# Batch 2's first two head pairs turned by transposing transfers instead of TensorE, in an attention and mixer kernel

## The chip, the cores and the metric

The kernel runs on one core of a Trainium2 chip. The metric is the device time of one execution in microseconds. The core has TensorE (PE; its weight loads are listed as PEld), VectorE (DVE), ScalarE (ACT), GpSimd (POOL) and SyncE (SP). In this kernel POOL issues the loads from memory, which also turn float32 into bfloat16, and SP issues stores, small copies and transposing transfers.

## The reference

The reference is causal attention with a decay bias, followed by a mixer block. There are 8 batches, 8 heads, 576 positions and 64 channels per head.

```python
scores = scale * np.matmul(q, k.transpose(0, 1, 3, 2))
cum = np.cumsum(np.maximum(s, 0.0), axis=-1)
bias = -(cum[:, :, :, None] - cum[:, :, None, :])
scores = np.where(causal, -1000000000.0, scores + np.minimum(bias, 0.0))
attn = softmax(scores)
x = np.matmul(attn, v)                # then heads side by side: (8, 576, 512)
...
h = x.transpose(0, 2, 1) @ U @ V      # U (576, 32), V (32, 576)
u = x + h.transpose(0, 2, 1)
out = u + np.maximum(u @ w_ch1, 0.0) @ w_ch2    # (512, 2048), (2048, 512)
```

## The kernel before

The 64 heads are worked off in 32 pairs (n = 0 to 31), four pairs to a batch; pair n belongs to batch n // 4. For each pair q and k have to stand with the 64 channels on partitions. They are put into a tile of `slots`, with four more rows that carry the running sums of s, so that one matmul yields scores and bias together. `slot_of` names the tile: for pairs 8 and up it is (n + 1) % 3 of the first three, so pair 8 uses slots[0] and pair 9 slots[1], which pairs 5 and 6 used before.

The words of the order are these. T is the filling of a slot, S the scores with their exponentials, V the product with v and its normalisation, M the low-rank mixing of a batch, F a step of the channel mixer, and D a transposing transfer of a pair. The channel mixer (`chanmix`) runs as `fill`: after most steps of attention `step_fill` gives it a turn, at a pace. PE and POOL run in the order of the program text (`in_program_order` at the end); the order on VectorE, ScalarE and SP is set by it up to the first batch and by the planner after that.

There are two ways to fill a slot.

- `transposes` (L301): q and k of a batch were loaded by `load_qk` (L128) with 72 partitions, in pieces of 512 numbers, into one of the two operand tiles `qk_sd` (even batches the first, odd ones the second). PE turns each pair with 16 matmuls against the identity (L316: two heads, q and k, four pieces) into PSUM, and four copies (L335) spread the result into the slot. `copies` gives some of them to ScalarE: of pairs 8 and 9, those of the first head.
- `turn_pair` and `part_pair` (L349, L358): `load_pair` (L117) brings q and k of one pair with 96 partitions, in four loads of pieces of 64 numbers, into a quarter of the second operand tile (`of_pair`). `turn_pair` has SP issue a transposing transfer (L350) into one of three `landings`: a tile of its own called `turned`, the rest of the second operand tile, and the head of the first one. Then it calls `load_pair` for the pair four further on. `part_pair` copies the two halves of the landing into the slot on VectorE (L362).

In both, from batch 1 on, `rows_of` has SP fetch the bias rows into the slot by two small transfers (L296) ahead of the rest.

`ZP` is the first pair that goes the second way: 10 before. So batch 2's pairs 8 and 9 are loaded by `load(2)` (heads 0 to 3 into the first operand tile, which batch 0 has left) and turned by PE; pairs 10 and up go through transfers. The words around it (L1240 on):

```python
weave("S5 T6 S5 F T6 S5 F S5 S6 T7 S6 T7 S6 S6")
for n in range(ZP, ZP + PB):
    load_pair(n)
weave("V4 V4 S7 V5 S7 V5 S7 V6 S7 V6 T8 T8 V7 S8 V7 S8 T9 S8 T9 D10")
weave("S8 S9 M1 S9 D11 M1 S9 D12 M1 M1 S9 M1 F M1")
```

The last PE reads of the second operand tile as batch 1's operand are those of T7, so the loads of a pair into it wait for them.

Of the kernel before, what the change touches and what calls it, by code (L numbers as in the profile page):

```python
# [41 lines left out]
def kernel(  # L42
# [15 lines left out]
    B, H, S, D = q.shape  # L58
# [7 lines left out]
    NP = BH // 2  # L66
    PB = NP // B
# [2 lines left out]
    KA = D + 4  # L70
    NF = FF // 128
    FT = 2
    ZB, ZP = 3, 10
    TR, RT = 96, 6

    consts = ctx.enter_context(tc.tile_pool(name="consts", bufs=1))
# [10 lines left out]
    def pwork():  # L87
        return ps_w.tile([128, 512], FP32, tag="w", name="pwork")
# [17 lines left out]
    qk_sd = [consts.tile([128, 2 * H * TT * D], BF16, name=f"qk_sd{i}") for i in range(2)]  # L106
    QK = 2 * PB * RT * 128

    def alloc_qk(b):
        q_t[b], k_t[b] = qk_sd[b % 2][:TP].rearrange("p (c h x) -> c p h x", c=2, h=H)  # L110

    def of_pair(n):
        return qk_sd[ZB % 2][:TR, ds(n % PB * QK // PB, QK // PB)].rearrange(
            "p (c t two d) -> p c t two d", c=2, t=RT, two=2
        )

    def load_pair(n):  # L117
        b, hp = divmod(n, PB)
        for hh in range(2):
            for c, src in enumerate((q, k)):  # L120
                nc.gpsimd.dma_start(  # L121
                    out=of_pair(n)[:, c, :, hh, :],
                    in_=src[b, 2 * hp + hh].rearrange("(t p) d -> p t d", p=TR),
                )

    def load_qk(b, h, n):
        for dst, src in ((q_t[b], q), (k_t[b], k)):
            nc.gpsimd.dma_start(  # L128
                out=dst[:, ds(h, n), :],
                in_=src[b, ds(h, n)].rearrange("h (p t) d -> p h (t d)", p=TP),  # L130
            )
# [32 lines left out]
    def init_v(eng, vt):  # L164
        eng.memset(vt[64:, 4, :, :], 0.0)
        eng.memset(vt[:, 0:4, :, D : D + 1], 1.0)
        eng.memset(vt[0:64, 4, :, D : D + 1], 1.0)

    def v_slot(b):
        return v_slots[b % 3 if b < 3 else 2 - b % 2]  # L170

    def load_v(b, parts=range(5)):
        vt = v_slot(b)
        if 0 < b < 3:
            init_v(nc.gpsimd, vt)
        for t in parts:
            rows_t = 128 if t < 4 else 64
            nc.gpsimd.dma_start(  # L178
                out=vt[:rows_t, t, :, 0:D],
                in_=v[b, :, ds(t * 128, rows_t), :].rearrange("h p d -> p h d"),  # L180
            )
# [10 lines left out]
    def slot_of(n):  # L192
        return slots[n % NSLOT if n < 2 * PB else (n + 1) % 3]
# [93 lines left out]
    def copies(n, hh, par):  # L287
        b = n // PB
        on_act = hh == (n in (4, 7)) and (
            n in (0, 4, 7, 8, 9) or (n, par) == (1, 0)  # L290
        )
        return nc.scalar.copy if on_act else nc.vector.tensor_copy

    def rows_of(n):
        for r, n_r, c in ((0, 3, 1), (3, 1, 0)):
            nc.sync.dma_start(  # L296
                out=slot_of(n)[ds(D + r, n_r), :, ds(c * S, S)],
                in_=rows_hbm[ds(r, n_r), ds(2 * n, 2)],
            )

    def transposes(n):  # L301
        b, hp = divmod(n, PB)
        slot = slot_of(n)
        if b > 0:
            rows_of(n)
        tps = {}

        def turn(hh, c):
            if c == 0:
                tile = pwork()  # L310
                tps[hh] = tile.bitcast(BF16)[:, : 2 * 4 * TP].rearrange(
                    "p (c t m) -> p c t m", c=2, t=4
                )
            src = (q_t[b], k_t[b])[c]
            for t2 in range(4):
                nc.tensor.transpose(  # L316
                    tps[hh][:, c, t2, :],
                    src[:, 2 * hp + hh, ds(t2 * 128, 128)],
                    identity[:TP, :TP],
                )  # L320

        if b == 0:
            for hh in range(2):
                turn(hh, 0)
            yield
        for hh in range(2):
            if b > 0:
                turn(hh, 0)
            turn(hh, 1)
            tp = tps[hh]  # L330
            dst = slot[0:D, hh, 0 : 2 * S]
            for par in range(2):
                src = tp[par * D : par * D + D]
                in_turn = dst.rearrange("p (c m t two) -> p c m t two", c=2, t=4, two=2)
                copies(n, hh, par)(in_turn[:, :, :, :, par], src.rearrange("p c t m -> p c m t"))  # L335
            yield
# [7 lines left out]
    def last_sp():  # L344
        return [ins for ins in list(nc.cur_bb.bb.instructions) if ins.engine == E.SP][-1]
# [3 lines left out]
    def turn_pair(n):  # L349
        nc.sync.dma_start_transpose(  # L350
            out=landing(n).rearrange("p (a m) -> p a m", m=TR),
            in_=of_pair(n).rearrange("p c t two d -> p (c t two d)"),
        )
        after(tc, last_sp(), x_turned[-1])
        if n < NP - PB:
            load_pair(n + PB)
# [728 lines left out]
    def step_fill():  # L1085
        pace[0] += pace[1]
        if pace[0] < 16:
            return
        pace[0] -= 16
        if NG - 3 in expanded and not ps_tail:  # L1090
            return
        while fill:
            if next(fill[0], fill) is not fill:
                return
            fill.pop(0)
# [9 lines left out]
    def fill_with(n):  # L1105
        per, pace[1] = pace[1], 16
        for _ in range(n):
            step_fill()
        pace[1] = per


    def pT_of(n):
        if n < PB + 3:
            return pTs[n % 2] if n % PB < 2 else pT_early[n % PB - 2]
        return pTs[(n + 1) % 2]

    def step(*gens):
        for gen in gens:
            next(gen, None)
# [75 lines left out]
    load_v(1)  # L1195
    load_w2(1)

    def load(b):
        alloc_qk(b)
        load_qk(b, 0, 4)  # L1200

    load(2)
    load_v(2)
    fill.append(chanmix(0, first_hT, 4))
    pace[1] = 0
    made = {}

    def weave(order):
        for word in order.split():
            if word == "F":  # L1210
                fill_with(1)
                continue
            kind, n = word[0], int(word[1:])
            if kind == "D":
                x_turned.append(last_sp())
                turn_pair(n)
                x_turned.pop()
                continue
            if word not in made:
                if kind == "T":  # L1220
                    made[word] = transposes(n)
                elif kind == "S":
                    made[word] = scores(n, pT_of(n))
                elif kind == "V":
                    made[word] = values(n, pT_of(n))
                else:
                    made[word] = seqmix(n)
            step(made[word])
            step_fill()
# [8 lines left out]
        nc.vector.tensor_copy(V_end[ds(dt * R, R), dt, :], V_sb[:R, 512:S])  # L1238
    pace[1] = 7
    weave("S5 T6 S5 F T6 S5 F S5 S6 T7 S6 T7 S6 S6")  # L1240
    for n in range(ZP, ZP + PB):
        load_pair(n)
    weave("V4 V4 S7 V5 S7 V5 S7 V6 S7 V6 T8 T8 V7 S8 V7 S8 T9 S8 T9 D10")
    weave("S8 S9 M1 S9 D11 M1 S9 D12 M1 M1 S9 M1 F M1")
    fill.append(chanmix(1))
    pace[1] = 11
    for n in range(2 * PB, NP + 2):
        b, hp = divmod(n, PB)
        if hp == 0 and b + 1 < ZB:
            load(b + 1)  # L1250
        if ZP + 3 <= n + 3 < NP:
            turn_pair(n + 3)
        mixing = seqmix(b - 1) if hp == 1 and b > FT else iter(())
        if b == B:
            fill_with(3)
            for _ in range(3):
                step(mixing)
                fill_with(2)
        if n > 2 * PB and n + 1 < NP:
            for at, _ in enumerate((transposes if n + 1 < ZP else part_pair)(n + 1)):  # L1260
                step_fill()
                if at == 1:
                    step(mixing)
        if 2 * PB + 1 < n < NP:
            for at, _ in enumerate(scores(n, pT_of(n))):
                relu_by[0] = E.DVE if hp == 1 and at == 2 else E.Activation
                step_fill()
                relu_by[0] = E.Activation
                if at == 1:
                    step(mixing)  # L1270
        for _ in mixing:
            fill_with(1)
        if hp == 1 and FT < b < B:
            fill.append(chanmix(b - 1))
            pace[1] = 12 if b < 6 else 10
        if 2 * PB < n <= NP:
            run(values(n - 1, pT_of(n - 1)))
        if 2 <= b < B - 1:
            if b + 1 < ZB:
                load_v(b + 1, range(5 if hp == 0 else 0))  # L1280
            else:
                load_v(b + 1, ((0, 1), (2,), (3,), (4,))[hp])
# [70 lines left out]
```

## Time and profile before

| | |
|---|---|
| median of 3 runs | 348.08 us (347.5 to 348.23) |
| profiled execution | 348.07 us, its span 346.4 us |
| granted TensorE clock | 1.0 |
| PE transposes, L316 | 160 weight loads (98 ns) and 160 matmuls (198 ns) |
| copies from PSUM, L335 | 29 on VectorE (803 ns), 11 on ScalarE (801 ns) |
| copies from a landing, L362 | 44 on VectorE (455 ns) |
| transposing transfers of pairs, L350 | 22, SP busy with issuing one for 1.28 to 3.10 us |
| loads of pairs on POOL, L121 | 88 of 72 KB, issued in 0.73 us each, median 4.3 to 4.4 us to landing |

The span is the time from the first to the last instruction of the program; the time of an execution has 1.7 us more around it. The transposes' lengths overlap in the engine: four groups of eight of them belong to pairs 8 and 9. "To landing" is the time from the issue of a transfer until its data has arrived.

### The profile page before, as it was taken

To read this page: it belongs to the slowest core of one execution; us is meant where nothing else is said; L and a number is where in the kernel's file an instruction comes from. 1 tells how busy PE (TensorE), PEld (TensorE's weight loads), DVE (VectorE), ACT (ScalarE), POOL (GpSimd) and SP (SyncE) were. 2 spreads that over 40 slices of the span, in tenths; PEclk is the share of its full clock that TensorE was granted. 3 is DMA by queue.
4 is the path that set the end of the run, shared out by engine and by line. 5 is a ranking of instruction groups with operands and counts; after the bars stand their busy time and mean duration, and the time that the engine had idled before them with its cause. 6 is when DMAs were issued, how large, how long until landed. Compare 5 with 4: busy or idle time off the path is not lost.

```text
span 346.4 us, 8956 instructions
## 1 busy us (share of the span) xinstructions
PE 336.5 (97%) x3623; PEld 243.8 (70%) x3657; DVE 259.3 (75%) x576; ACT 205.2 (59%) x310; POOL 123.6 (36%) x179
## 2 busy tenths in 40 slices
PE   8999999999999999999999999999999999999996
PEld 4585656655688558865678558865687558888885
DVE  8884756779799558974898459965989597875774
ACT  4886985838850886168724874378462546675710
POOL 7997454839476337322933274000000000000000
PEclk9999999999999999999999999999999999999999
DMA  7999999999999999999999999583025343010022
GB/s 106 159 179 207 186 186 120 129 204 189 154 162 174 202 126 127 114 206 151 124 116 168 163 135 143 117 177 76 2 70 122 69 83 71 32 61 32 30 93 91
DMA packets 166529, 43.79 MB, mean 126 GB/s; under 512 B 151129, under 2 KB 164857, under 8 KB 166489
## 3 DMA queue, kind: packets, MB, share of 16 engines
q0 software_dynamic: 97456, 18.44, 73.7%
q1 hardware_dynamic: 68744, 24.60, 35.7%
q8 instruction: 28, 0.46, 0.6%
q10 hardware_dynamic: 288, 0.20, 0.2%
q14 instruction: 13, 0.10, 0.1%
HBM read 37.25 MB, written 9.70 MB: 136 GB/s over the span
## 4 chain that ended last, share of the span: by engine, by line
PE 78%; DVE 9%; ACT 3%; issue 3%; DMA 3%; POOL 2%; DVEq 0%; ACTq 0%
PE pwork L662 23%; PE pwork L720 13%; PE quarter L720 10%; PE pscore L428 9%; PE pwork L492 7%; PE parts L952 6%; PE pwork L681 3%; DMA w_sb<-in_moe_w_ch_dram 3%; DVE uT L547 2%; DVE slot L698 1%; DVE o_sb L734 1%; POOL v_slot L178 1%; PE pscore L662 1%; ACT pT L446 1%; PE pwork L952 1%
## 5 line engine op out<-in xcount | busy, mean ns | idle before, releaser
L662 PE MATMUL pwork<-uT,w_sb 128*128 128x512 bf16 x407 | 104.2, 379 | 1.9 <-ACT pT L464 0.5
L1044 ACT ACTIVATE hT<-pwork 128x512 bf16<-128x512 f32 x107 | 64.7, 610 | 37.4 <-PE pwork L662 36.6
L446 ACT ACTIVATE pT<-pscore 128x1024 bf16<-128x1024 f32 x57 | 57.5, 1030 | 49.3 <-PE pscore L428 49.2
L662 PEld LDWEIGHTS <-w_sb 128*128 128x128 bf16 x448 | 39.1, 98 | 39.2 <-issue 1.0
L121 POOL DMA_DIRECT2D qk_sd<-in_q_dram x44 | 32.6, 740 | 75.4 <-DMA qk_sd<-qk_sd 48.4
L428 PE MATMUL pscore<-slot 68*128 68x128 bf16 (+1 forms) x506 | 55.9, 246 | 0.6 <-DMA slot<-hT 0.2
L428 PEld LDWEIGHTS <-slot 68*128 68x128 bf16 x570 | 42.0, 97 | 18.2 <-DMA slot<-hT 0.8
L720 PEld LDWEIGHTS <-hT 128*128 128x128 bf16 x496 | 46.8, 98 | 7.1 <-DVE uT L547 0.5
L372 DVE TENSOR_TENSOR pT<-pT,keep 128x512 bf16<-128x512 bf16 (+1 forms) x81 | 28.5, 353 | 28.7 <-ACT pT L446 22.4
L492 PEld LDWEIGHTS <-pT 128*128 128x128 bf16 x870 | 32.4, 98 | 6.1 <-issue 0.9
L492 PE MATMUL pwork<-v_slot,pT 128*128 128x65 bf16 x870 | 35.4, 193 | 0.2 <-DVE uT L547 0.2
L178 POOL DMA_DIRECT2D v_slot<-in_v_dram x40 | 34.5, 875 | 2.9 <-DMA w_sb<-in_moe_w_ch_dram 2.3
L121 POOL DMA_DIRECT2D qk_sd<-in_k_dram x44 | 32.4, 736 | 2.6 <-DMA v_slot<-in_v_dram 1.4
L502 DVE TENSOR_TENSOR x_sb<-pwork,rec 128x320 bf16<-128x320 f32 x64 | 31.1, 488 | 1.4
L458 ACT ACTIVATE pT<-pscore 128x1024 bf16<-128x1024 f32 x29 | 30.3, 1045 | 2.1 <-PE pscore L428 2.0
L720 PE MATMUL pwork<-w_sb,hT 128*128 128x256 bf16 x240 | 29.9, 272 | 0.0
L720 PEld LDWEIGHTS <-slot 128*128 128x128 bf16 x256 | 24.1, 98 | 4.1 <-issue 1.1
L335 DVE COPY slot<-pwork 64x576 bf16<-64x576 bf16 x29 | 23.3, 803 | 4.5 <-PE pwork L316 3.2
L501 DVE RECIPROCAL rec<-pwork 128x5 f32<-128x5 f32 x64 | 12.0, 188 | 12.8 <-PE pwork L492 12.4
L720 PE MATMUL pwork<-w_sum,slot 128*128 128x256 bf16 x160 | 20.1, 272 | 0.3 <-DVE o_sb L734 0.3
L720 PE MATMUL quarter<-w_sb,hT 128*128 128x256 bf16 x144 | 18.0, 273 | 0.3 <-DVE uT L547 0.3
L965 DVE TENSOR_TENSOR hT<-pT,parts 128x512 bf16<-128x512 f32 x16 | 10.8, 682 | 6.3 <-PE parts L952 3.6
(164 smaller groups left out, 491.4 us busy)
## 6 DMA issues: line engine op xcount, KB each, us to landing
out_dram<-o_sb SPq DMA_DIRECT2D x34, 256.0 KB
v_slot<-in_v_dram POOLq DMA_DIRECT2D x32, 128.0 KB, 6.6
w_sb<-in_moe_w_ch_dram POOLq DMA_DIRECT2D x4, 1024.0 KB, 13.5
qk_sd<-in_q_dram POOLq DMA_DIRECT2D x44, 72.0 KB, 4.4
qk_sd<-in_k_dram POOLq DMA_DIRECT2D x44, 72.0 KB, 4.3
qk_sd<-in_q_dram POOLq DMA_DIRECT2D x3, 288.0 KB, 10.5
qk_sd<-in_k_dram POOLq DMA_DIRECT2D x3, 288.0 KB, 10.7
qk_sd<-in_q_dram POOLq DMA_DIRECT2D x4, 144.0 KB, 4.8
```

Of the source, the lines that this page charges most:

```text
L121: nc.gpsimd.dma_start(out=of_pair(n)[:, c, :, hh, :], in_=src[b, 2 * hp + hh].rearrange("(t p) d -> p t d", p=TR),)
L178: nc.gpsimd.dma_start(out=vt[:rows_t, t, :, 0:D], in_=v[b, :, ds(t * 128, rows_t), :].rearrange("h p d -> p h d"),)
L372: nc.vector.tensor_tensor(dst, dst, keep[:, :, 0:w].to_broadcast([128, n_tiles, w]), op=ALU.min)
L428: nc.tensor.matmul(dst, lhsT=slot[0:KA, hh, ds(S + j * 128, 128)], rhs=slot[0:KA, hh, lo:hi], start=True, stop=True,)
L446: nc.scalar.activation(pT[:, hh, 0:1024], near, EXP, scale=scale)
L458: nc.scalar.activation(pT[:, :, 1024:1536], mid.rearrange("p (a b) -> p a b", a=2), EXP, scale=scale)
L492: nc.tensor.matmul(po[:, i, :], lhsT=pT[:, hh, ds(place(j, i), 128)], rhs=vt[:, j, h, :], start=(j == 0), stop=(j == i), skip_group_check= ...
L502: nc.vector.tensor_tensor(x_sb[:, hp, :, ds(hh * D, D)], po[:, :, 0:D], rec.to_broadcast([128, 5, D]), op=ALU.mult,)
L662: nc.tensor.matmul(f1, lhsT=w1_sb[:, kt, ds(nf * 128, 128)], rhs=u[:, kt, :], start=(kt == 0), stop=(kt == 3),)
L720: nc.tensor.matmul(acc[:, i, :], lhsT=a[:, kt, ds(i * 128, 128)], rhs=b[:, kt, :], start=(begin and i == 0 and kt == 0), stop=(kt == HF - ...
L952: nc.tensor.matmul(acc[:, i, :], lhsT=w[:, kt, ds((2 * e + i) * 128, 128)], rhs=m[:, kt, :], start=(begin and i == 0 and kt == 0), stop=(k ...
L1044: nc.scalar.activation(hT[:, nf, :], f1, RELU)
```

## The change

`ZP` becomes 8, so pairs 8 and 9 also go through `load_pair`, `turn_pair` and `part_pair`. Pair 8 is loaded into a place in the first operand tile (behind the first 1152 columns, which are a landing), pair 9 into its quarter of the second. `load(2)` is gone and `load_pair(8)` stands in its place; batch 2's v load moves from there to behind `load_pair(9)`, after T7. The loads of pairs 12 and 13, which stood in a loop, are now called by D8 and D9. D8 stands at the head of the order and D9 between the two steps of T8. The landings rotate by two places, since they count from `ZP`.

```diff
-    ZB, ZP = 3, 10
+    ZB, ZP = 3, 8
...
     def of_pair(n):
-        return qk_sd[ZB % 2][:TR, ds(n % PB * QK // PB, QK // PB)].rearrange(
-            "p (c t two d) -> p c t two d", c=2, t=RT, two=2
-        )
+        if n == ZP:
+            place = qk_sd[(ZB + 1) % 2][:TR, ds(2 * S, QK // PB)]
+        else:
+            place = qk_sd[ZB % 2][:TR, ds(n % PB * QK // PB, QK // PB)]
+        return place.rearrange("p (c t two d) -> p c t two d", c=2, t=RT, two=2)
...
         on_act = hh == (n in (4, 7)) and (
-            n in (0, 4, 7, 8, 9) or (n, par) == (1, 0)
+            n in (0, 4, 7) or (n, par) == (1, 0)
         )
...
-    def load(b):
-        alloc_qk(b)
-        load_qk(b, 0, 4)
-
-    load(2)
-    load_v(2)
+    load_pair(ZP)
...
-                    made[word] = transposes(n)
+                    made[word] = (transposes if n < ZP else part_pair)(n)
...
-    for n in range(ZP, ZP + PB):
+    load_pair(ZP + 1)
+    load_v(2)
+    for n in range(ZP + 2, ZP + PB):
         load_pair(n)
-    weave("V4 V4 S7 V5 S7 V5 S7 V6 S7 V6 T8 T8 V7 S8 V7 S8 T9 S8 T9 D10")
+    weave("D8 V4 V4 S7 V5 S7 V5 S7 V6 S7 V6 T8 D9 T8 V7 S8 V7 S8 T9 S8 T9 D10")
...
-        if hp == 0 and b + 1 < ZB:
-            load(b + 1)
-        if ZP + 3 <= n + 3 < NP:
+        if 2 * PB + 2 <= n < NP - 3:
             turn_pair(n + 3)
```

The order of the instructions on the engines is that of before but for this: PE has 32 weight loads and matmuls fewer, ScalarE four copies fewer, VectorE four copies of another kind in place of four (and one mask and one output sum beside them change places), POOL eight loads of pairs 8 and 9 in place of two of batch 2, ahead of batch 2's v loads, and SP two transposing transfers more. On SP, D8 stands ahead of the bias rows of pair 8, D9 between those of pairs 8 and 9, and D10 right behind the rows of pair 9, as before.

## The prediction

> **What bounds the kernel now.** I read the busy shares of the page first, then PE's order of time around batch 2's first head pairs, then the chain of waits there, then the queues that would have to feed the new path.
>
> ```profile
> span 346.4 us, 8956 instructions
> PE 336.5 (97%) x3623; PEld 243.8 (70%) x3657; DVE 259.3 (75%) x576; ACT 205.2 (59%) x310; POOL 123.6 (36%) x179
> ```
>
> PE is busy for 336.5 of 346.4 us, so whatever leaves PE's queue shortens the span, and whatever makes PE wait lengthens it: only 9.9 us of idle time exist in all, spread over the whole span, and nothing later can absorb a stall. The granted clock is full throughout. PE's own order of time shows what the change takes away:
>
> ```profile
> 57.49 0.62 PE L492 MATMUL pwork<-v_slot,hT 128*128 128x65 bf16 x15
> 57.95 0.43 PE L316 MATMUL pwork<-identity,qk_sd 72*128 72x72 bf16 x8
> 58.20 1.03 PE L681 MATMUL pwork<-w_sb,hT 128*128 128x512 bf16 x4
> 59.07 0.42 PE L316 MATMUL pwork<-identity,qk_sd 72*128 72x72 bf16 x8
> 59.33 0.62 PE L492 MATMUL pwork<-v_slot,pT 128*128 128x65 bf16 x15
> 60.08 0.62 PE L428 MATMUL pscore<-slot 68*128 68x128 bf16 x6
> ...
> 63.39 0.42 PE L316 MATMUL pwork<-identity,qk_sd 72*128 72x72 bf16 x8
> 63.65 0.60 PE L428 MATMUL pscore<-slot 68*128 68x320 bf16 x4
> ...
> 64.95 0.42 PE L316 MATMUL pwork<-identity,qk_sd 72*128 72x72 bf16 x8
> 65.21 0.23 PE L428 MATMUL pwork<-slot 68*128 68x64 bf16 x2
> ```
>
> The first column is the start, the second the length (ends overlap, so costs are read from start to next start). The four L316 groups are the transposes of pairs 8 (57.95, 59.07) and 9 (63.39, 64.95). The scores of pair 8 start at 60.08. The chain of waits says why:
>
> ```profile
> 58.43 0.79 issue
> 59.22 0.82 ACT slot L335
> 60.04 0.05 issue
> 60.08 0.62 PE pscore L428 x6
> ```
>
> The 15 matmuls at 59.33 need 0.46 us (57.49 to 57.95), so PE could have gone on at 59.79; it waited 0.29 us for ScalarE's second copy out of PSUM.
>
> Now the feeding side. The weight load ahead of batch 2's operands, the wait it causes on POOL, and the first transposing transfer of before (pair 10) on SP:
>
> ```profile
> 36.84 0.89 POOL L263 DMA_DIRECT2D w_sb<-in_moe_w_ch_dram  x1 [1.03 <-DMA qk_sd<-in_q_dram]
> 37.76 0.75 POOL L128 DMA_DIRECT2D qk_sd<-in_q_dram  x1
> 42.09 0.72 POOL L128 DMA_DIRECT2D qk_sd<-in_k_dram  x1 [3.58 <-PE pwork L662]
> 52.28 0.73 POOL L121 DMA_DIRECT2D qk_sd<-in_q_dram  x1 [3.97 <-DMA w_sb<-in_moe_w_ch_dram]
> ...
> 63.38 1.57 SPq L350 DMA_TRANSPOSE turned<-qk_sd  x1
> 65.06 1.36 SPq L296 DMA_DIRECT2D slot<-rows_hbm  x2
> 69.87 5.06 SPq L350 DMA_TRANSPOSE qk_sd<-qk_sd  x2
> ```
>
> The reader is to see a queue that runs ahead of its data: the weights issued at 36.84 land 14.9 us later, at 51.74, and POOL's next loads wait for such landings. From 42 to 63 us every POOL load that waits starts 0.2 to 0.8 us after the landing of the eighth load before it, so eight are in flight at most.
>
> **The change, part by part.**
>
> PE loses 32 transposes. Their four groups take 0.25 (57.95 to 58.20), 0.26, 0.26 and 0.26 us: 1.03 us. The rest of PE's order is unchanged, instruction by instruction, so this is a full gain. The 0.29 us wait for ScalarE's copy goes too. Without any new wait PE reaches pair 8's scores at 60.08 - 0.29 - 0.51 = 59.28 us.
>
> ScalarE loses four copies of 0.80 us. VectorE swaps four copies of 0.803 us for four of 64x1152 from SBUF (median 0.455). Both engines wait for PE in this stretch (3.39 of 5 us busy on ScalarE, 3.58 on VectorE from 55 to 60 us), so I count nothing for them.
>
> The new wait is in front of pair 8's scores. Its chain: load of pair 8, transposing transfer D8, a VectorE copy; and the bias rows of pair 8, which stand behind D8 on SP.
>
> - The load. Its four transfers (576 pieces each, 72 KB) take the place of the two big ones at 37.76 and 42.09, so they are issued by about 44.8 us and stand in the queue behind the weights that land at 51.74. The 2304 pieces then need between 1.0 us (pair 10's four loads, the same shape, landed between 62.2, where the load before them landed, and 63.2) and 3.2 us (batch 2's v loads, 1024 pieces each, landed 1.44 us apart). Batch 1's v loads, right behind a weight load as here, ran 4096 pieces in 4.85 us, so 2.7 us. Pair 10's pieces had mostly moved while one late part of the v load was awaited; so I stay near 2.7 and take 2.5: landed at 54.2 (52.7 to 54.9).
> - D8. SP issued pair 10's transfer 0.16 us after its load landed (63.22, 63.38), and by the semaphore records it landed at 68.21, 4.83 us later. Over the other pairs the same transfer took between 3.4 us (issued 163.39) and 7.6 us (issued 69.87, behind output stores in SP's own queue). At 54.4 SP's queue holds nothing else and loads of 128-byte pieces run beside it, as at 63.38, so I take 4.83: landed at 59.2.
> - The first copy, 0.46 us: 59.7. The bias rows behind D8: pair 10's second one had moved its last packet at 68.60, 5.2 us after that transfer's issue, so 59.6 here; hidden by the copy.
>
> Pair 8's scores start at 59.7 instead of 59.28: a new wait of 0.4 us, from nothing (all ends early) to 3.4 us (both late: 54.9 + 0.2 + 7.6 = 62.7). Behind the waiting copies on VectorE stand the normalisation of pair 7's values and an output sum, which PE doesn't need before it has passed the scores itself. Behind D8 on SP stand rows 8, D9, rows 9, D10 and the first output stores. D9 is issued after rows 8, at 54.4 + 1.6 + 1.4 = 57.4 and after its load (four loads behind pair 8's, about 57), lands at 62.2 by D10's latency and at 65.0 by the longest; pair 9's scores come at 66.14 - 1.3 + 0.4 = 65.2, so its cover is 2.5 us with the copy counted and the cost nothing; at the longest latency 0.3 us.
>
> POOL: pair 9's load waits for PE's last reads of batch 1 (47.3), and batch 2's v loads, issued from 43.98 before, wait behind it until about 54. They are read at 75.07, some 11 us after they would land. Pair 10's load ends about 3 us later than at 58.2; D10 then lands near 70, and its copies are at 75.02: cover of 5 us, nothing counted. Pair 13's load now waits for D9, pair 14's for D10 as before; their transfers go out from 82.44 on, so nothing is due.
>
> A row on the loads: pair 10's four took 10.1, 8.3, 6.2 and 5.7 us from issue to landing, yet landed within 0.9 us of each other (62.4 to 63.2). The Trainium skill, "DMA: Bandwidth & Descriptors", Anatomy of one DMA, speaks against the change here: it fits each transfer of this kind with a fixed 2.0 us and a part by bytes, which is an estimate of 2.2 us for 72 KB. Paid one after the other that would be 8.7 us for pair 8's four, a landing at 60.4, a wait of 6.6 us and 353.4 us in all. Pair 10's landings show the fixed parts overlapping, so I give this 0.01 within the slow case below.
>
> Sum: 1.03 + 0.29 - 0.4 = 0.9 us. The profiled execution took 348.07 us (span 346.4 and 1.7 around it), the median of the runs 348.08; so 348.07 - 0.9 = 347.2 us. Without a new wait it is 346.75.
>
> **Rivals.**
>
> The gain is eaten (no change). The load at 3.2 us and D8 at 5.3 (as issued at 102.08): 51.74 + 3.2 + 0.2 + 5.3 + 0.5 = 60.9, a wait of 1.6 us: 348.07 - 1.32 + 1.6 = 348.4. For it: two late steps are each ordinary in the trace. Against it: each wants something beside it on the queue that isn't there at 54 us.
>
> D8 takes the place of the transposes as PE's bound (slower). It shares the transfer engines with pair 9's load and the v loads, which the change has moved to just this time, and takes the 7.6 us of the transfer at 69.87: 54.4 + 7.6 + 0.5 = 62.5, a wait of 3.2 us, net +1.9: 349.95. It decides from a wait of 2.0 us on, that is, a D8 of 6.4 us. For it: the next four pair transfers (issued 69.87, 72.84, 82.44, 87.56) took 6.8 to 7.6 us. Against: those stood behind another transposing transfer or stores in SP's own queue; the lone one took 4.83. The Trainium skill, same page, "Queues, rings and completion order", says that each engine goes round between the queues it has work for, packet by packet; by that alone loads would lengthen D8, which is this rival.
>
> The gain isn't there because PE wasn't the bound. PE's chain holds 78% of the span and the stretch has no other long wait; I give this no share of its own.
>
> **How the numbers follow.** A measurement of this kernel can tell 0.2%, 0.7 us. Wait under 0.6 us (faster): 0.50. Wait between 0.6 and 2.0 us, or 0.3 us at pair 9 too (347.4 to 348.8): 0.22. A wait above 2.0 us (348.8 to 351): 0.28, with what I haven't seen in a stretch where four queues change their order. Likeliest: 347.2, its own range 346.7 to 347.4. The range 346.5 to 349.4 leaves out the upper half of the slow case (0.13) and a little below.
>
> **What would show it.** Four L316 groups gone from PE; pair 8's load landing near 54.2, D8 issued near 54.4; pair 8's scores at 59.3 to 59.9, with VectorE's copy or the rows as the releaser; pair 9's scores without a wait; all later stages earlier by the same 0.9 us. Wrong if PE idles over 1.3 us before pair 8's or pair 9's scores, or if a later pair waits for its copies.

## The result and the profile after

| | before | after |
|---|---|---|
| median of the runs | 347.94 us (347.48 to 348.8) | 349.2 us (347.78 to 353.72) |
| ratio after / before | | 1.0046, interval 1.0031 to 1.006 |
| profiled execution, its span | 348.07 us, 346.4 us | 353.14 us, 351.4 us |

The forecast was 347.2 us and faster; the kernel became 1.3 us slower by the medians (1.1 to 2.1 us by the interval). The profiled execution of the changed kernel is the second longest of its 22 and lost more than a median run, so the readings below name places, and sizes come from the medians.

The head of the page, to be held against that of before:

```profile
span 351.4 us, 8902 instructions
PE 337.6 (96%) x3591; PEld 244.1 (69%) x3625; DVE 259.8 (74%) x576; ACT 202.2 (58%) x306; POOL 127.7 (36%) x185
```

PE has its 32 matmuls fewer and still a longer span: 13.8 us idle instead of 9.9, and 337.6 us busy where some 335.5 were due (336.5 less the 1.03 us of the transposes), because part of it ran at half clock (below).

SP's queue in order of time (start, time that the issue took):

```profile
53.90 1.40 SPq L352 DMA_TRANSPOSE turned<-qk_sd  x1
55.40 1.44 SPq L298 DMA_DIRECT2D slot<-rows_hbm  x2
57.05 1.83 SPq L352 DMA_TRANSPOSE qk_sd<-qk_sd  x1
58.98 1.56 SPq L298 DMA_DIRECT2D slot<-rows_hbm  x2
66.86 1.49 SPq L352 DMA_TRANSPOSE qk_sd<-qk_sd  x1
...
73.14 1.84 SPq L352 DMA_TRANSPOSE turned<-qk_sd  x1
75.17 3.08 SPq L352 DMA_TRANSPOSE qk_sd<-qk_sd  x1
```

The rows are D8, pair 8's bias rows, D9, pair 9's bias rows, D10, D11, D12. D8 and D9 go out as forecast, 0.5 us earlier even. But D10 goes out at 66.86 instead of 63.38, D11 at 73.14 instead of 69.87, D12 at 75.17 instead of 72.84.

PE where pair 8's scores begin (the square bracket is PE's idle time and what ended it):

```profile
58.63 0.62 PE L494 MATMUL pwork<-v_slot,pT 128*128 128x65 bf16 x15
60.71 0.60 PE L430 MATMUL pscore<-slot 68*128 68x128 bf16 x6 [1.47 <-DMA slot<-rows_hbm]
```

D8 landed at 59.17 and VectorE's copies were done at 60.22, but PE waited until 60.71 for the bias rows that stand behind D8 on SP. The wait of 1.47 us alone is more than the forecast gain of 1.32.

VectorE and PE later on, two places in two fences:

```profile
81.56 0.92 DVE L364 COPY slot<-turned 64x1152 bf16<-64x1152 bf16 x2 [2.28 <-DMA turned<-qk_sd]
```

```profile
86.48 1.04 PE L664 MATMUL pwork<-uT,w_sb 128*128 128x512 bf16 x4 [0.68 <-DVE x_sb L504]
...
112.11 0.19 PE L494 MATMUL pwork<-v_slot,pT 128*128 128x65 bf16 x1 [1.63 <-DMA v_slot<-in_v_dram]
112.14 1.66 PE L722 MATMUL pwork<-w_sb,hT 128*128 128x256 bf16 x8
```

At 79.28 VectorE reached pair 11's copies, and D11 had not landed (81.53). VectorE works in order, so the normalisations behind that copy came late and PE waited for x_sb until 86.48. Until 112.11 PE waited 1.63 us for the last piece of batch 3's v. The eight matmuls right behind it take 1.66 us where eight of this shape take 1.03 to 1.05 in the 20 us before.

The chain of waits, from the second half of w2 to that last piece of v, shows how the two places hang together (start, length, what):

```profile
37.19 14.75 DMA w_sb<-in_moe_w_ch_dram
57.58 7.61 DMA v_slot<-in_v_dram
65.47 2.12 POOL qk_sd L123 x3
67.89 1.44 POOL qk_sd L123 x2
69.33 3.71 DMA qk_sd<-in_q_dram
73.14 8.39 DMA turned<-qk_sd
82.09 1.36 POOL qk_sd L123 x2
83.52 1.43 POOL qk_sd L123 x2
84.95 6.04 DMA qk_sd<-in_q_dram
91.00 8.62 DMA turned<-qk_sd
100.17 1.36 POOL qk_sd L123 x2
101.62 1.43 POOL qk_sd L123 x2
103.05 9.01 DMA v_slot<-in_v_dram
112.30 1.50 PE pwork L722 x8
```

Hardly any of it is engine work; in the kernel before, PE held most of this stretch up to 101 us. Read link by link: batch 2's v, issued from 54.11 on (43.98 before), landed by 65.18, and pair 10's load behind it at 66.71 instead of 63.23, so D10 went out 3.5 us later. The load of pair 15 (82.09) waited for D11's landing, as each load waits for the transposing transfer four pairs before; the load of pair 18 (100.17) waited for D14's; and batch 3's last piece of v (103.05, before 98.13) stands behind it in POOL's queue. Two links are only inferred and don't hold: the loads named ahead of D11 and D14 are those of later pairs and landed at 73.27 and 92.14, after the issue. D11's and D14's own loads had landed at 70.27 and 82.21; these transfers stood in SP's queue, which from D10 on runs some 3 us late as a block (D13 at 85.43 instead of 82.44, D14 at 91.00 instead of 87.56). So in this execution a delay of 3 us at 67 us was handed on by both queues to 112 us. Not all of it is lateness of issue: D13 and D14 also took longer themselves (7.87 and 8.62 us from issue to landing; 6.77 and 7.14 before).

How much earlier or later PE is than in the profiled execution of before, at the first product with v of a pair (in both kernels the same matmul; us, worked out from the traces):

| pair (time before) | 6 (56.1) | 7 (59.3) | 8 (75.1) | 10 (89.3) | 12 (108.7) | 13 (116.3) | 31 (268.5) |
|---|---|---|---|---|---|---|---|
| after | -0.19 | -0.71 | +0.30 | +1.15 | +1.16 | +4.57 | +4.67 |
| e10, engines' work alone | -0.39 | -0.91 | -1.59 | -1.59 | -1.58 | -1.59 | -1.93 |
| e13, rows first and order | -0.35 | -0.87 | -1.73 | -1.73 | -1.73 | -1.74 | -2.13 |
| e14, transfers alone, rows first | -0.09 | -0.09 | -0.09 | -0.10 | -0.10 | -0.10 | -0.13 |

The first row falls by 0.5 with half of the transposes gone, then rises at the three places named. Behind pair 13 it stays: the second half of the kernel gives nothing back and takes nothing.

### The profile page after: what moved, and what is told of

It reads as the page before. It is cut to its first block, busy times and chain, and to the rows that moved or that the text cites. A ratio compares the mean times of both kernels' runs of the same rounds, so it can differ in the third digit from the quotient of the medians.

```text
span 351.4 us, 8902 instructions
## 1 busy us (share of the span) xinstructions
PE 337.6 (96%) x3591; PEld 244.1 (69%) x3625; DVE 259.8 (74%) x576; ACT 202.2 (58%) x306; POOL 127.7 (36%) x185
## 4 chain that ended last, share of the span: by engine, by line
PE 58%; DMA 21%; POOL 9%; DVE 7%; issue 3%; ACT 2%; POOLq 0%; DVEq 0%; SPq 0%
PE pwork L664 17%; PE pwork L722 12%; PE quarter L722 10%; PE parts L954 6%; DMA qk_sd<-in_q_dram 6%; PE pscore L430 5%; PE pwork L494 5%; DMA turned<-qk_sd 5%; DMA v_slot<-in_v_dram 5%; DMA w_sb<-in_moe_w_ch_dram 4%; POOL qk_sd L123 3%; POOL v_slot L180 2%; DMA xT<-x_sb 1%; DVE uT L549 1%; PE pwork L954 1%
## 5 line engine op out<-in xcount | busy, mean ns | idle before, releaser
L123 POOL DMA_DIRECT2D qk_sd<-in_q_dram x48 | 35.3, 735 | 73.7 <-DMA qk_sd<-qk_sd 39.6
L123 POOL DMA_DIRECT2D qk_sd<-in_k_dram x48 | 35.9, 748 | 8.8 <-PE pwork L664 3.4
L494 PE MATMUL pwork<-v_slot,pT 128*128 128x65 bf16 x870 | 36.2, 194 | 2.3 <-DMA v_slot<-in_v_dram 2.1
L337 DVE COPY slot<-pwork 64x576 bf16<-64x576 bf16 x25 | 20.1, 802 | 2.9 <-PE pwork L318 1.2
L364 DVE COPY slot<-qk_sd 64x1152 bf16<-64x1152 bf16 x32 | 16.1, 504 | 1.4 <-DMA qk_sd<-qk_sd 1.1
```

What stands on the lines that cost most here:

```text
L123: nc.gpsimd.dma_start(out=of_pair(n)[:, c, :, hh, :], in_=src[b, 2 * hp + hh].rearrange("(t p) d -> p t d", p=TR),)
L494: nc.tensor.matmul(po[:, i, :], lhsT=pT[:, hh, ds(place(j, i), 128)], rhs=vt[:, j, h, :], start=(j == 0), stop=(j == i), skip_group_check= ...
```

## The experiments

Two theories stood against each other. By the first, the loss is in the waits of pairs 8 and 9 and in the slide behind batch 2's v load, and moving the rows or the v load mends it. By the other, the transfer queues themselves have no slack: whatever the two new pairs bring to them is handed on to later transfers. Times are medians; the kernel before ran on the same chip each time.

**e1, the changed kernel again,** nothing edited.

> The changed kernel once more, for a second profile and its spread. If the loss is one late v transfer that tips over in some executions (theory A), this profile shows either full clock with a span near 347, a wait of about 1.5 us before pair 8's scores and none of batch 3's values on v, or the half-clock stretch of 3.4 us and a span above 349. If the loss is in the wait before pair 8's scores alone (rival C), the time moves with that wait and nothing else changes from profile to profile.

Measured: 349.6 us beside 347.66; ratio 1.0054, interval 1.0019 to 1.0088. PE's order of time in its profile:

```profile
60.39 0.60 PE L430 MATMUL pscore<-slot 68*128 68x128 bf16 x6 [0.73 <-DMA slot<-rows_hbm]
...
67.87 0.60 PE L430 MATMUL pscore<-slot 68*128 68x128 bf16 x6 [1.79 <-DMA slot<-rows_hbm]
```

The result stands, but the time is lost at other places: now pair 9's rows, behind D9, cost most, and nothing waits for v. One trace of this kernel does not tell where it usually loses.

**e2, batch 2's v load behind the loads of pairs 10 and 11.**

```diff
     load_pair(ZP + 1)
-    load_v(2)
     for n in range(ZP + 2, ZP + PB):
         load_pair(n)
+    load_v(2)
```

> Batch 2's v load put behind the loads of pairs 10 and 11 on POOL instead of in front of them; all else as changed. Theory A (v's five transfers hold up pair 10's load, so D10, and behind it on SP D11 and D12, start 3 us late, and POOL with all its later loads slides with them): D10 issued before 64 instead of 66.9, D11 near 70, no wait of pair 11's copies, batch 3's last v transfer landed near 104, full clock; the wait before pair 8's scores stays near 1.5 us; 348.1 us, spread like before. Rival B (two transposing transfers and six more loads are what slows the queues, wherever v stands): as changed, 349.2 with a spread of some 6 us.

Measured: 347.95 beside 347.66; 1.0017, interval 0.9994 to 1.0039. In the profile D10 goes out at 60.21 and D11 at 69.37, and only pair 8 makes PE wait (0.79). Better than the changed kernel, no better than before.

**e3, the bias rows of pairs 8 and 9 ahead of D8 and D9 on SP.**

```diff
             if kind == "D":
                 x_turned.append(last_sp())
+                if n < ZP + 2:
+                    rows_of(n)
                 turn_pair(n)
...
     def part_pair(n):
-        rows_of(n)
+        if n >= ZP + 2:
+            rows_of(n)
```

> The bias rows of pairs 8 and 9 put ahead of D8 and D9 on SP; POOL as changed. Theory A: pair 8's scores then wait for VectorE's copy, at 59.7 to 59.8 instead of 60.7, a wait of 0.6 us instead of 1.5, so 0.9 us less in front; the late slide on POOL stays, so the time is near 348.3 with the wide spread. Rival C (the wait before pair 8 is the loss): 347.9 or less with the spread of before.

Measured: 348.25 beside 347.66; 1.0024, interval 1.0002 to 1.0045. PE's order of time:

```profile
59.67 0.61 PE L431 MATMUL pscore<-slot 68*128 68x128 bf16 x6 [0.74 <-DVE slot L365]
66.09 0.61 PE L431 MATMUL pscore<-slot 68*128 68x128 bf16 x6 [0.73 <-DVE slot L365]
```

Now the releaser is VectorE's copy, as the prediction had it, and each of the two pairs costs 0.7 us. Their sum, 1.47 us, is more than the gain.

**e4, e2 and e3 together.**

> Batch 2's v load behind the loads of pairs 10 and 11, and the rows of pairs 8 and 9 ahead of D8 and D9. Theory A (the loss is waits: before pair 8's scores, and from loads that slid behind the v load): pair 8's scores at 59.7, 0.4 us earlier than with v alone, pair 9's without a wait, full clock: 347.3 to 347.6 against 347.7 before. Rival B (the queues have too much to move): between the two single edits or no better than either, 348, with runs above 350 left.

Measured: 352.9 beside 347.81; 1.0108, interval 1.0062 to 1.0154. There is no wait at pairs 8 and 9, and it is far worse than either theory had it. VectorE, then PE:

```profile
96.09 0.92 DVE L365 COPY slot<-qk_sd 64x1152 bf16<-64x1152 bf16 x2 [4.70 <-DMA qk_sd<-qk_sd]
```

```profile
100.04 0.61 PE L723 MATMUL pwork<-w_sum,slot 128*128 128x256 bf16 x4 [1.30 <-DVE slot L701]
102.94 0.69 PE L525 MATMUL pwork<-U_sb,x_sb 128*128 128x32 bf16 x20 [2.30 <-DVE x_sb L505]
```

D13 landed at 96.06 (89.21 before), VectorE stood for 4.70 us, and PE waited twice for what stood behind that copy. D10 was issued at 61.86, 5 us earlier than in the changed kernel, but took 11.78 us beside batch 2's v load (issued 59.53 to 63.74) and landed at 73.64, 1.7 us later than there; D13 took 9.63. So an earlier issue did not bring an earlier landing, and the loss came out at D13. This is where the first theory fell.

**e6, e4 with pair 8's load also ahead of the second half of w2,** and **e7, e4 with PE's order changed** (both steps of V7 ahead of S8, one step of M1 ahead of pair 9's second scores).

```diff
+    load_pair(ZP)
     load_w2(1)
-    load_pair(ZP)
```

```diff
-T8 V7 S8 V7 S8 T9 S8 T9 D10  |  S8 S9 M1 S9 D11
+T8 V7 V7 S8 S8 T9 S8 T9 D10  |  S8 M1 S9 S9 D11
```

> Both of these, and pair 8's load put ahead of the second half of the second weights on POOL. Theory A: pair 8 landed near 47.5, no wait before its scores, D10 and D11 as in e2, full clock: 348.0 - 1.3 = 346.7 us. Rival B: the slide remains and the time stays above 348. It loses if the weights, 3 us later (54.6), come after the matmuls that read them (55.2).

> As e4, and PE's words around the two waits changed places: both halves of pair 7's values ahead of pair 8's scores, and the first step of batch 1's mixing ahead of pair 9's. PE then reaches pair 8's scores about 1.0 us later with the same work done. Theory A: no wait before pair 8's or pair 9's scores, a gain of the whole 1.0 to 1.3 us: 346.5 to 346.9. Rival B: the slid loads make other waits (pair 11, 12 or batch 3's v) and the time is 347.7 or more.

Measured: e6 352.93 beside 347.66 (1.0128, interval 1.0087 to 1.017), e7 351.98 beside 347.81 (1.0139, interval 1.0102 to 1.0176). In e6, D8 went out at 49.17 and landed only at 59.47, beside the weights; so issuing early didn't help. e7's profiled execution took 347.86 us with no PE wait above 0.3 us at pairs 8 to 13, but its other five runs took 350.17 to 354.76 us.

**e8, pair 8 left on TensorE and pair 9 alone moved,** on two chips; **e9, e8 with the v load behind the loads of pairs 10 and 11.**

```diff
-    load_pair(ZP)
+    alloc_qk(2)
+    load_qk(2, 0, 2)
...
-made[word] = (transposes if n < ZP else part_pair)(n)
+made[word] = (transposes if n <= ZP else part_pair)(n)
```

> Half of the change: pair 8 is turned by PE again, from two loads of 144 KB, pair 9 by a transfer; batch 2's v load stays where the change put it. Theory A: no wait before pair 8's scores (0.3 us for ScalarE's copy as before), 0.5 us gained there, and less to load ahead of pair 10, so the slide is 1 to 2 us instead of 4: 347.2 to 348. Rival B: half the extra traffic, half the loss: 348.6.

> The version with pair 8 left on PE and pair 9 by transfer once more, on this chip: 347.5 beside 347.9 for the kernel before (half of PE's gain, 0.5 us, no wait); theory 'a delay handed on' allows up to 349 in single runs when pair 9's traffic meets a late load.

> The same half, with batch 2's v load behind the loads of pairs 10 and 11. Theory A: half the gain and no late wait: 347.2. Rival B: no different from e8.

Measured: e8 347.48 beside 347.81 (0.9995, interval 0.998 to 1.001) and 347.94 beside 347.81 (1.0003, interval 0.9994 to 1.0012): the same as before. Neither profile has a PE wait at pairs 9 to 13 that the kernel before has not. The second theory had half the loss here, 348.6, and that missed. e9 took 352.71 beside 347.81 (1.0145, interval 1.0128 to 1.0161), with D13 landing at 94.54 and PE waits of 1.68, 1.22 and 1.44 us that ended between 101 and 113 us; the last is for batch 3's v, as in the changed kernel. Neither theory had put e9 there (347.2, or as e8). The edit that sets e9 apart from e8 is the later v load, so that is what costs here; why it costs in e4 and e9 and not in e2 is not shown.

**e10 and e11, the two halves of the change apart.** e10 has the work of the changed kernel on PE, VectorE and ScalarE and the transfers of before; it leaves out D8 and D9, and its copies of pairs 8 and 9 read other numbers that lie in the first operand tile. e11 is the reverse: PE turns batch 0's last pair instead, and nothing reads D8 and D9.

```diff
 e10, from the kernel before
-made[word] = transposes(n)
+made[word] = (transposes if n < 8 else part_stale)(n)
+    def part_stale(n):
+        rows_of(n)
...
+                    slot_of(n)[0:D, hh, 0 : 2 * S], qk_sd[0][0:D, ds((n - 8) * 1024, 2 * S)]
 e11, from the changed kernel
-        src = (q_t[b], k_t[b])[c]
+        src = (q_t[b % 2], k_t[b % 2])[c]
-made[word] = (transposes if n < ZP else part_pair)(n)
+made[word] = transposes(n)
```

> The engines' work of the changed kernel with the transfers of the kernel before: batch 2's loads and the order of POOL and SP stay as before, there are no transposing transfers for pairs 8 and 9, PE's 32 transposes are gone, and the four VectorE copies fill the slots of pairs 8 and 9 with other numbers that lie in the first operand tile at that time (so these two pairs' scores come from wrong operands). Both theories (waits only at pairs 8 and 9; a delay handed on along the transfer queues): the gain on the engines stands, 1.0 to 1.3 us, so 346.6 to 346.9 beside 347.9 for the kernel before. If PE were not the bound here, 347.9, the third rival of the prediction.

> The transfers of the changed kernel with the engines' work of the kernel before: loads, transposing transfers and the order of POOL and SP are those of the changed kernel, but nothing reads D8's and D9's landings; PE's 32 transposes and the eight copies out of PSUM are back and turn batch 0's last pair, which still lies in the first operand tile (so the scores of pairs 8 and 9 come from wrong operands). Theory 'waits only at pairs 8 and 9': nothing waits for D8 and D9, only the bias rows of pair 8 behind D8 can cost 0.5 us, so 348.0 to 348.4. Theory 'a delay handed on along the queues': D10 is issued near 67, the last piece of batch 3's v lands at 109 to 112, PE waits there or at pairs 12 and 13 and loses a stretch of clock in part of the runs: 349.0 to 351, at least as slow as the changed kernel.

Measured: e10 346.62 beside 347.81 (0.9967, interval 0.9955 to 0.9979), e11 348.82 beside 347.81 (1.0036, interval 1.0015 to 1.0057). PE in e10, at pair 8:

```profile
58.43 0.62 PE L502 MATMUL pwork<-v_slot,pT 128*128 128x65 bf16 x15
59.04 0.61 PE L438 MATMUL pscore<-slot 68*128 68x128 bf16 x6
```

The engines' half is worth 1.19 us; its runs lie close together (346.14 to 347.44). The transfers' half costs 1.0 us though nothing reads D8 and D9. But e11 did not separate what it was to separate, since pair 8's rows still stood behind D8, which took 7.57 us here:

```profile
61.99 0.96 PE L430 MATMUL pscore<-slot 68*128 68x128 bf16 x6 [1.81 <-DMA slot<-rows_hbm]
```

**e12, batch 3's last pieces of v called earlier.**

```diff
-load_v(b + 1, ((0, 1), (2,), (3,), (4,))[hp])
+parts = ((0, 1), (2,), (3,), (4,)) if b > 2 else ((0, 1), (2, 3, 4), (), ())
+load_v(b + 1, parts[hp])
```

> The changed kernel with the last two pieces of batch 3's v load called one and two pairs earlier (all three later pieces by pair 9), so that they go ahead of the loads of two pairs on POOL. Theory 'a delay handed on': the v pieces land by about 105, the wait of 1.63 us at 112 and the stretch at half clock behind it are gone, and what is left is the wait at pair 8: 347.8 to 348.5; if the delay only moves to the pair loads that are now behind the v pieces, 349 or more, with a wait at the copies of pairs 14 to 16. Theory 'waits only at pairs 8 and 9': as the changed kernel, 349.2.

Measured: 349.2 beside 347.81; 1.0049, interval 1.0027 to 1.0071, just as slow as the changed kernel. The wait for v at 112 us is gone; in its place D14 lands at 101.28, VectorE waits 1.93 us for it, and PE waits until 103.20 (0.88) and 110.17 (1.21) for two results of VectorE, uxT and uT; at pair 8 it waits 0.97 for the rows. The loss at the later places moved to the pair loads that are now behind.

**e13 to e16, the waits of pairs 8 and 9 taken away, then traffic taken away.** e13 is e3 with e7's order of PE, batch 2's v load where the change has it. e14 is e11 with SP's order of e13. e15 is e13 without batch 3's v load, e16 the kernel before without it.

> The changed kernel with the bias rows of pairs 8 and 9 ahead of D8 and D9 on SP, and two words of PE's order changed so that other work covers what is left: both steps of V7 ahead of S8, one step of M1 ahead of pair 9's second scores. Batch 2's v load stays where the changed kernel has it. PE then doesn't wait before pairs 8 and 9 (0 to 0.4 us). Theory 'waits only at pairs 8 and 9': 346.6 to 347.0. Theory 'a delay handed on': D10 is issued at 66 to 67 as in the changed kernel, PE waits once or twice between 85 and 112 us in part of the runs: median 347.6 to 349.5.

> The transfers of the changed kernel with the engines' work of before, as in the run before, but with the bias rows of pairs 8 and 9 ahead of D8 and D9, so that PE waits for nothing that the new transfers bring to these two pairs (their scores come from batch 0's last pair). Theory 'waits only at pairs 8 and 9': as the kernel before, 347.8. Theory 'a delay handed on': 348.2 to 350, with waits between 80 and 115 us.

> The run before the last (rows first, order changed, D8 and D9 read) without batch 3's v load (five transfers, 4608 pieces of 128 bytes; batch 3 then uses batch 1's v, so its output is wrong). Theory 'a delay handed on': the later loads and transposing transfers find the queue emptier, no wait is left, 346.5 to 347.0, clearly below the same kernel with the load. Theory 'waits only at pairs 8 and 9': no different from the same kernel with the load.

> Control: the kernel before without batch 3's v load (its output is wrong in batch 3). Nothing waits for that load in the kernel before, so both theories: 347.8, as the kernel before, within 0.3 us.

| | median (lowest to highest) | ratio to before (interval) |
|---|---|---|
| before | 347.82 (347.49 to 356.4) | |
| e13, both halves, no wait at pairs 8, 9 | 348.03 (346.33 to 353.25) | 0.9988 (0.9959 to 1.0018) |
| e14, transfers' half alone | 348.84 (347.89 to 354.46) | 1.0017 (0.999 to 1.0045) |
| e15, e13 without batch 3's v | 347.85 (346.52 to 349.54) | 0.9979 (0.9946 to 1.0011) |
| e16, before without batch 3's v | 347.77 (347.48 to 350.35) | 0.9988 (0.9958 to 1.0017) |

e13's profiled execution, 346.33 us, has the whole gain and no new wait: the third row of the table of shifts. But its median is 1.4 us above e10's, which has the same work on the engines. e14's ratio is unclear, since its interval includes no loss at all; of its runs 9 of 12 are above 348.28 us, of the kernel before 5 of 35. So by the medians the transfers cost about 1 us also with no wait at pairs 8 and 9; that they cost something is likely from the spread of the runs, and the size is rough. For e15 the second theory had expected 346.5 to 347.0, and that missed: the v load is not what the delay needs. Its profile shows VectorE, then PE:

```profile
93.33 0.92 DVE L365 COPY slot<-qk_sd 64x1152 bf16<-64x1152 bf16 x2 [1.56 <-DMA qk_sd<-qk_sd]
```

```profile
100.18 0.69 PE L525 MATMUL pwork<-U_sb,x_sb 128*128 128x32 bf16 x20 [0.63 <-DVE x_sb L505]
```

It is the place of e4 again: D13, VectorE's copy, x_sb. But here most of D13's lateness is not handed on by the queue. SP issues D13 in the kernel before and in e13:

```profile
82.44 1.88 SPq L350 DMA_TRANSPOSE turned<-qk_sd  x1
82.61 2.13 SPq L352 DMA_TRANSPOSE qk_sd<-qk_sd  x1
```

The issue is 0.17 us later (1.61 in e14, 1.07 in e15), and the landing 2.16 us (3.59 and 4.10): D13 took 6.77 us from issue to landing before, and 8.76, 8.75 and 9.79 in e13, e14 and e15. Why it takes longer there isn't shown. How long a landing lies before the first of its copies on VectorE (us, from the semaphore records; 0.1 or less means that VectorE waited or nearly did; e1's is large because PE itself is 3.4 us behind by then):

| | before | e10 | after | e1 | e8 (two) | e12 | e13 | e14 | e15 |
|---|---|---|---|---|---|---|---|---|---|
| D11 | 1.45 | 0.70 | 0.02 | 1.92 | 3.92, 3.27 | 0.09 | 0.91 | 0.11 | 0.29 |
| D13 | 3.60 | 2.58 | 0.66 | 2.72 | 3.58, 3.29 | 0.22 | 0.02 | 0.02 | 0.02 |

**e17 and e18, VectorE's copies of pairs 10 to 15 behind the scores of the pair before instead of ahead of them,** on e13 and on the kernel before. The other engines' order is the same.

```diff
-for at, _ in enumerate(part_pair(n + 1)):
+late = part_pair(n + 1, n + 1 < 16)
+for at, _ in enumerate(range(2) if n + 1 < 16 else late):
...
+if n > 2 * PB and n + 1 < 16:
+    drain(late)
```

> Rows first and order changed as in the fastest version so far, and in addition the copies of pairs 10 to 15 stand behind the scores of the pair before in VectorE's order instead of ahead of them, some 4 us later; the order of the other engines is the same. If the delay is handed to PE by VectorE's waiting copies (rec, x_sb, uxT behind a copy whose landing is late), the slack of D11 and D13 grows from under 1 us to 3 to 5 us and the runs come together near 346.3 to 347.0, faster than both kernels. If the delay reaches PE another way (v, xT), 348.0 as without this edit. If PE now waits for the later copies themselves, 349.

> Control: the kernel before with the same later place of the copies of pairs 10 to 15 in VectorE's order. D11 and D13 land 1.45 and 3.6 us before their copies there, and PE waits for none, so 347.8, as the kernel before, within 0.3 us.

Measured: 349.9 beside 347.68 (1.0073, interval 1.0051 to 1.0096) and, for the control, 350.31 (1.007, interval 1.0057 to 1.0083), where 347.8 was expected. The slack grew as meant (D11 6.00, D13 4.72 us in e17), but both kernels lost 2 us or more. PE in the control:

```profile
86.43 1.04 PE L663 MATMUL pwork<-uT,w_sb 128*128 128x512 bf16 x4 [1.09 <-DVE x_sb L503]
```

The copies now stand right in front of the normalisations, and PE waits for those with every landing in time. It tells nothing more of the delay, but it says that VectorE's order has no room for this mending: 0.9 us of copies in the wrong place cost PE as much as a late landing.

No version here that computes the whole beats the kernel before by more than the measurement is uncertain.

## Why the prediction was wrong

- **The gain** was right. Forecast 1.03 + 0.29 = 1.32 us; e10 measured 1.19 (0.7 to 1.6 by its interval), so PE is the bound there.
- **Pair 8's load and D8** were right in the profiled execution: D8 at 53.90 and landed at 59.17, forecast 54.4 and 59.2; its 5.27 us lay near the 4.83 taken. In e1 it took 5.15. The slower rival had D8 take 7.6 us: that did not come about in the changed kernel's two profiles, but D8 took 7.57 in e11 and 7.00 in e7.
- **The new wait before pair 8** was mis-sized: forecast 0.4 us, 1.47 measured, 0.73 in e1. The step was "so 59.6 here; hidden by the copy": pair 8's rows behind D8 came at 60.7, not 59.6, and set the start.
- **Pair 9, "the cost nothing"**, held in the profiled execution and failed in e1 (1.79 us) and e3 (0.73). Pair 9's rows stand behind D9 in the same way, and D9 took 8.55 us in the profiled execution, 9.53 in e1; the longest that the prediction reckoned with was 7.6.
- **The step that failed with the largest cost** is "D10 then lands near 70, and its copies are at 75.02: cover of 5 us, nothing counted", with its neighbour "so nothing is due". The later load was forecast, and D10 did keep its cover (71.95, 3.4 us ahead of its copies). But I followed it to one reader only. D11 stands behind D10 in SP's queue and had 1.45 us of slack, D13 had 3.60. In the profiled execution SP's queue kept the delay as a block, and POOL took it over, since its loads wait for landings; in e13 to e15 D13 itself took 2 to 3 us longer. A price for either stood nowhere in the sum.
- **The sizes**, from medians, each against the kernel before on its own chip: the engines' work alone gains 1.19 us (e10); with the transfers, but the waits at pairs 8 and 9 covered, the kernel is 0.21 above before (e13), so about 1.4 is lost behind these pairs, where the forecast had nothing; with the waits it is 1.26 above, so they cost about 1.05, where the forecast had 0.4. e13's interval is 2 us wide, so the split is rough.
- **The signs of being wrong** that the prediction named came: PE was idle over 1.3 us before pair 8's scores (1.47) and, in e1, pair 9's (1.79). Of the other, a later pair that waits for its copies, something near it came: pair 11's copies waited for D11, and PE for what stood behind them.
- **The rival "gain eaten"** named the right size for the first part (a wait of 1.6 us) by the wrong reason (load and D8 both late).
- **Four readings** were off by little. The weights landed at 51.71, not 51.74; batch 1's v loads ran in 4.94 us, not 4.85; batch 2's v loads landed 1.5 us apart (57.24 to 61.81), not 1.44, which makes the load's upper bound 3.4 us instead of 3.2; and the shortest transposing transfer of a pair took 3.24 us (issued 234.34), not 3.4. None moves the forecast by more than 0.1 us.

What stays open: in which place the 1.4 us between e13's median and e10's are lost, and why the transposing transfers take longer in some of these kernels. The profiled executions of e13 and e14 (346.33 and 348.35 us) show no new PE wait. D13's copy, x_sb and PE are shown in e4 and e15, D11's in after, D14's in e12, batch 3's v in after and e9; how the runs divide among them isn't shown.

## What to carry to other kernels

When a change gives a queue more to carry, follow the delay through every transfer behind it in the queue, and through every queue that waits for one of those, up to the first reader whose slack is smaller than the delay; the cover of the next reader says nothing of the one after it. Allow too for later transfers taking longer than they did (D13: 6.77 us before, up to 9.79 here). Read slack as landing to first use, not as the idle share of an engine: here 1.45 us at D11 was all there was. Try the two halves of a change apart (work without transfers, transfers without work): that gave the gain a size that several mendings had not, and a control for each edit (e18) kept a wrong fix from being read as a finding.

## What the hardware showed

A PE wait of 1.6 to 1.9 us can cost twice. The windows around the wait of the changed kernel (stretch; length, busy time of PE, PEld, DVE, ACT, POOL; granted clock; the busy share of the transfer engines as the view adds it up, and GB/s):

```profile
109.00:112.39 3.39, 1.52 (x25) 1.19 (x23) 2.42 (x7) 0.00 (x0) 1.37 (x2) 1.00 2.10 171
112.39:115.80 3.41, 3.41 (x30) 2.67 (x28) 2.11 (x6) 0.00 (x0) 3.37 (x5) 0.50 2.14 196
115.80:119.00 3.20, 3.15 (x28) 2.22 (x28) 2.72 (x6) 1.51 (x3) 0.40 (x1) 1.00 2.10 204
```

After the wait PE ran at half clock for 3.413 us, worth 1.7 us more. The same stretch followed waits of 1.79 us (e1), 1.81 (e11) and 1.89 (e16, at 13.09); after 1.47 us (after), and after 1.68 us in e9, there was none. The Trainium skill, "TensorE: Matmul & The Clock Gate", Part 1: The HAM clock gate, gives a free-running window of 3413 ns, and the length agrees; it speaks of a drop after about 3.4 us of idling, and here about half of that was enough, in some executions and not in others. Eight of the nine runs of the changed kernel above 350 us show a mean clock of 0.995, about one such stretch.

The loads also move less while a transposing transfer moves. By the packet records of the changed kernel, while D10's 1152 packets moved (68.50 to 71.27) the loads moved 320 packets per us, against some 900 in the 2 us before and in the 2 us behind. In the kernel before, D10's 1152 packets (65.03 to 67.19) had 373 beside them, 386 before and 914 behind, so not every lull around one is its doing. It fits that two more such transfers take time from the loads around them as well as their own; no run here sizes that.
